# Attention and FFN block on one core: the VectorE's exponentials as five-pass cubics, in place of sums of five shifted bf16 patterns, with the FFN weights resident

## The chip, the cores and the metric

The kernel runs on one core of a Trainium2 chip. The core has a matrix engine (TensorE, PE in the profile), a vector engine (VectorE, DVE), an activation engine (ScalarE, ACT), GpSimd (POOL), SyncE (SP), which here issues nearly all transfers, and 16 DMA engines. Engines run their own instruction streams in order and meet at semaphores. SBUF is the on-chip memory, PSUM the accumulators that the PE writes. The metric is the device time of one execution in microseconds.

## What is computed

One block of a conditioned transformer, 2048 tokens, width 512, 32 heads of 16, FFN width 1792, all in bf16:

```
sa, ca, ga, sb, cb, gb = split(silu(c) @ w_mod, 6)
h = layernorm(x) * (1 + ca) + sa
q, k, v = h @ wqkv                                  # per head: [2048, 16]
x = x + ga * (softmax(q k^T / 4) v) @ wo
h = layernorm(x) * (1 + cb) + sb
x = x + gb * ((gelu(h @ w_gate) * (h @ w_up)) @ w_down)
```

The scores are 32 heads by 2048 by 2048, so 134 million exponentials. In tiles of 128 keys by 512 queries that is 2048 tiles.

## The kernel before

The scores are made transposed, keys on the partitions. Queries come in six sets (`SETS`: four of 512, 512, 512 and 256 queries, two of 128). A unit is four heads (every second head of a block of eight) times one query set; four score tiles of one unit that the PE can make side by side are a round. `qk` writes score tiles into PSUM `ps_sc`, six banks used as two halves of three. One ACTIVATE then reads up to three tiles at once, takes the exponential and writes bf16 tiles into E, a ring of slots. `pv_mms` multiplies a round of four tiles by V with a column of ones appended (`vaug`), in four column tiles side by side, and accumulates a whole unit in `ps_pv`. The ones give the softmax denominators. At a unit's end (`unit_end`) DVE copies the sums to `osb`; the denominators go through DRAM (`scr_den`, `scr_rec`) with six transfers on SP, a reciprocal on DVE lies between, and a multiplication gives `onorm`.

No order is written out by hand: a planner in `stream` emits it. It models each engine's free time and each operation's readiness, and at each step chooses the next PE work: three (or two) score tiles for the free half of `ps_sc`, a PV round, a piece of "side" work (projections, output projection, FFN, all in `ps_mi`), or a filler matmul that keeps the PE active. Side work follows the list in `plan`, with a start and a due position in score tiles; `credit` is how far it is behind. DVE work is queued as tasks and taken when the model has DVE free.

On top of this DVE makes exponentials of some score tiles. When the group of three has room and DVE is near free, one of the three banks holds a tile for DVE and the ACTIVATE covers two. Before the change, whole rounds of four go to DVE. Q is scaled so that a score is 65536 times the base-2 exponent. A single `tensor_scalar` from PSUM turns it into a uint16 that, read as bf16, is a piecewise linear power of two (`kq`), divided by five. `shift_task` adds four constants to these bits, one 2048-wide operation each (`sq`), which moves the joints of the linear pieces. The round then takes five PV passes: `kq` with `vaug`, and each shifted copy with `vs`, V scaled back by the shift. PSUM sums the five. Only rounds with key tiles from 12 on (`T0`) qualify, since `vs` holds no more. PV rounds may go out of order, and shift tasks have an urgency of their own.

SBUF is full with these buffers. So the FFN weights of the first four sets are streamed: `load` and `load_down` in `side_ffn` fetch 256-column blocks into two buffers each, on SP's queue, once per set. For the last sets `weight_parts` loads what remains resident, over the dead regions of qT, xs, dreg and mreg.

The split of a 128-column matmul into four 32-column tiles is in `mm` and is the same in both kernels:

```
if tp is None and int(rhs.ap[0][1]) == P and int(lhsT.ap[-1][1]) == P and mybir.dt.size(rhs.dtype) == 2:
    for j in range(4):
        self.mm(out[32 * j:32 * j + 32], lhsT[:, 32 * j:32 * j + 32], rhs, start, stop, (0, 32 * j))
```

Since all operations are recorded by helpers, the profile gives the helpers' lines: L309 is every matmul, L322 every ACTIVATE, L334 `tensor_scalar`, L339 `scalar_tensor_tensor`, L326 `tensor_tensor`, L343 copies, L372 every DMA. The groups are told apart by their tiles.

Of the kernel before, what the change touches and what calls it, by code (L numbers as in the profile page):

```python
# [13 lines left out]
P = 128  # L14
# [22 lines left out]
NSL = 12  # L37
assert NSL % CH == 0
LEAD = 5
T0 = 12  # L40
NK = 3
CREDIT = 1024
NS = 4
AHEAD = 24
FLOW = 4
URGENT = 9
LAG = 40
# [6 lines left out]
OCT = 65536.0  # L54
EXP_SCALE = float(np.log(2.0) / OCT)
Q_SCALE = float(0.25 * np.log2(np.e) * OCT)

SHIFT = (26, 51, 77, 102)
SHIFT_C = float(128 * (127 - np.log2(5) - 0.0565))
# [354 lines left out]
class _Kernel(_Recorder):  # L414
# [12 lines left out]
    def alloc(self):  # L427
# [8 lines left out]
        self.prodL = hreg[:, 0:NFC * 256].rearrange("p (f n) -> p f n", f=NFC)  # L436
# [6 lines left out]
        self.wst = [[mreg[:, 1024 * (2 * x + b):1024 * (2 * x + b) + 1024].rearrange("p (a n) -> p a n", a=NDC)  # L443
                     for b in range(2)] for x in range(2)]
        self.sq = [mreg[:, 4096 + 2048 * i:6144 + 2048 * i] for i in range(NS)]
        self.wmod = mreg[:, 0:NDC * 3072].rearrange("p (a n) -> p a n", a=NDC)
        dreg = sb("dreg", [P, NFC * D], BF16)
        self.tb1 = dreg[:, 0:8 * D].rearrange("p (b t n) -> p b t n", b=2, t=4)
        self.warm = dreg[:, 8 * D:9 * D]
        self.wdst = [dreg[:, a * D:(a + 2) * D] for a in (8, 10, 12)] + [mreg[:, a * D:(a + 2) * D] for a in (2, 0, 6, 4)]  # L450
        self.wdst = [a.rearrange("p (f n) -> p f n", f=2) for a in self.wdst]
        self.wg = [self.qT[:, :, 256 * i:256 * i + 256] for i in range(6)]
        self.wg.append(hreg[:, NFC * 256:NFC * 256 + 1024].rearrange("p (a n) -> p a n", a=NDC))
        self.wu = [self.wst[i // 2][i % 2] for i in range(4)]
        self.wu += [dreg[:, 1024 * i:1024 * i + 1024].rearrange("p (a n) -> p a n", a=NDC) for i in range(4, 7)]
        self.wd = [self.xs[:, 2 * i:2 * i + 2, :] for i in range(6)]
        self.wd.append(hreg[:, NFC * 256 + 1024:NFC * 256 + 2048].rearrange("p (f n) -> p f n", f=2))
        self.kq = [dreg[:, 0:2048], dreg[:, 2048:4096], mreg[:, 12288:14336]]
        self.vs = sb("vs", [P, len(SHIFT), NKT - T0, H * VW], BF16)
        self.wo = sb("wo", [P, 8, D], BF16)  # L460
        self.E = sb("E", [P, NSL, 512], BF16)
        self.onorm = sb("onorm", [P, 8, 512], BF16)
        self.ga = sb("ga", [P, D], BF16)
        self.gb = sb("gb", [P, D], BF16)
        self.xw = self.gw[:, 0, 0, 0:D]
# [11 lines left out]
        self.asum = self.rden[:, 0:2, 0:6]  # L477
        self.sc_bf = sb("sc_bf", [P, NDC], BF16)
        self.scbc = self.onorm[:, 0, :].rearrange("p (a n) -> p a n", a=NDC)
        self.modA = sb("modA", [P, 8], FP32)  # L480
        self.modB = sb("modB", [P, 8], FP32)
        self.rm4 = self.den[:, 0, 0:4]
        self.rm = sb("rm", [P, 2], FP32)
        self.ident = sb("ident", [P, P], BF16)
        self.ones = self.onorm[:, 1, 0:P]
# [8 lines left out]
    def prologue(self):  # L494
# [19 lines left out]
        self.memset(dve, self.ones, 1.0)  # L514
# [5 lines left out]
        self.memset(pool, self.rm4, 1.0)  # L520
        self.affine_select(self.rm4, [[-32, 4]], ALU.is_ge, 0.0, -16, 1)
        self.affine_select(self.rm4, [[32, 4]], ALU.is_ge, 0.0, 31, -1)
        self.reduce(self.rm[:, 1:2], self.rm4, mybir.AxisListType.X, ALU.add)
# [3 lines left out]
        for dc in range(NDC):  # L527
            self.mm(self.scp[:, 0, dc:dc + 1], self.crow[0:1, P * dc:P * dc + P], self.onorm[0:1, 1, 0:1])
# [28 lines left out]
    def act_stat(self, t):  # L557
        self.act(self.E[:, 0, :], self.xs[:, t, :], ACT.Copy, accum=self.asum[:, 0, t - 4:t - 3])
        self.act(self.E[:, 0, :], self.xs[:, t, :], ACT.Square, accum=self.asum[:, 1, t - 4:t - 3])
# [36 lines left out]
    def ln_norm(self, t, dst, src=None):  # L596
        self.ts("dve", dst, self.xs[:, t, :] if src is None else src, self.mv[:, t, 0:1], self.rstd[:, t:t + 1], ALU.subtract, ALU.mult)

# [89 lines left out]
    def side_v(self, g, dc):  # L688
        mi = self.mi[:, :]

        def part(t):
            for dci in range(NDC):
                self.mm(mi[:, P * t:P * t + P], self.hT[:, dci, 512 * g + P * t:512 * g + P * t + P],
                        self.wqkv[:, dci, 1024 + P * dc:1024 + P * dc + P],
                        start=(dci == 0), stop=(dci == NDC - 1))
        for t in range(4):
            yield 512, lambda t=t: part(t)
        dst = self.vaug[:, 4 * g:4 * g + 4, VW * 8 * dc:VW * 8 * dc + VW * 8]
        self.copy("dve", dst.rearrange("p t (h c) -> p t h c", c=VW)[:, :, :, 0:DH],
                  mi.rearrange("p (t h c) -> p t h c", t=4, c=DH))  # L700
        self.done(("v", g, dc))
        if 4 * g == T0 and not self.dry:
            c = slice(VW * 8 * dc, VW * 8 * dc + VW * 8)
            self.task([lambda i=i, o=o: self.ts("dve", self.vs[:, i, :, c], self.vaug[:, T0:NKT, c], float(2.0 ** (-o / 128)),
                                                None, ALU.mult) for i, o in enumerate(SHIFT)], ("vs", dc))
        yield END
# [60 lines left out]
    def side_mod(self):  # L767
        mi = self.mi[:, :]
        if not self.dry:
            self.task([lambda dc=dc: self.ts("dve", self.scbc[:, dc, :], self.ones, self.sc_bf[:, dc:dc + 1],  # L770
# [28 lines left out]
    def weight_parts(self):  # L799
# [3 lines left out]
        gv = self.B_w_gate.rearrange("(a p) n -> p a n", p=P)  # L803
        uv = self.B_w_up.rearrange("(a p) n -> p a n", p=P)
        dv = self.B_w_down.rearrange("(f p) n -> p f n", p=P)
        a = [part(self.wg[i], gv[:, :, 256 * i:256 * i + 256], "wg%d" % i) for i in range(7)]
        a += [part(self.wd[i], dv[:, 2 * i:2 * i + 2, :], "wd%d" % i) for i in range(7)]
        b = [part(self.wu[i], uv[:, :, 256 * i:256 * i + 256], "wu%d" % i) for i in range(7)]
        return a, b

    def up_w(self, w, fc, dci):
        return w[fc // 2][:, dci, P * (fc % 2):P * (fc % 2) + P]
# [15 lines left out]
    def normed(self, k, i):  # L828
        return self.E[:, NSL - 1, :] if k == len(SETS) - 1 else self.tb2[:, i, :]
# [5 lines left out]
    def wo_fin(self, bank, t):  # L835
        self.tt("dve", self.xw, bank, self.ga[:, :], ALU.mult)
        self.tt("dve", self.xs[:, t, :], self.xs[:, t, :], self.xw, ALU.add)

    def down_mm(self, bank, i, fc):
        self.mm(bank, self.prodL[:, fc, P * i:P * i + P], self.wd[fc // 2][:, fc % 2, :], start=(fc == 0), stop=(fc == NFC - 1))  # L840

    def down_fin(self, bank, t):
        self.tt("dve", self.xw, bank, self.gb[:, :], ALU.mult)
        self.tt("dve", self.xs[:, t, :], self.xs[:, t, :], self.xw, ALU.add)
        self.dma("sp", self.out[0, P * t:P * t + P, :], self.xs[:, t, :], "out%d" % (t % 4))

    def up_mm(self, bank, w, fc, c0, W, dci):
        self.mm(bank, self.up_w(w, fc, dci), self.t2T[:, dci, c0:c0 + W], start=(dci == 0), stop=(dci == NDC - 1))
# [35 lines left out]
    def side_ffn(self, gi, part=None):  # L884
# [6 lines left out]
        prod = self.prodT if W == 512 else self.prodL  # L891
        flow = gi < FLOW
# [6 lines left out]
        def load(x, ci):  # L899
            if flow and ci < len(chunks):  # L900
                v = (self.B_w_gate, self.B_w_up)[x].rearrange("(a p) n -> p a n", p=P)
                self.dma("sp", self.wst[x][ci % 2], v[:, :, 2 * P * ci:2 * P * ci + 2 * P], "st%d%d" % (x, ci % 2))

        def load_down(i):
            if flow:
                v = self.B_w_down.rearrange("(f p) n -> p f n", p=P)
                self.dma("sp", self.wdst[i], v[:, 2 * i:2 * i + 2, :], "sd%d" % i)

        yield from self.until(("ln2", gi))
        if flow:  # L910
            load(0, 0)
            load(1, 0)
        else:
            yield from self.until("weights")
        for h in range(2):
            yield from self.side_t(lambda t: self.normed(gi, t), n, h,
                                   lambda dc: self.t2T[:, dc, c0:c0 + W], self.modB)

        def up(x, ci, sub):
            for s, fc in enumerate(sub):  # L920
                for dci in range(NDC):
                    if flow:
                        lhs = self.wst[x][ci % 2][:, dci, P * (fc % 2):P * (fc % 2) + P]
                    else:
                        lhs = self.up_w((self.wg, self.wu)[x], fc, dci)
                    yield W, lambda s=s, lhs=lhs, dci=dci: self.mm(
                        mi[:, W * s:W * s + W], lhs, self.t2T[:, dci, c0:c0 + W], start=(dci == 0), stop=(dci == NDC - 1))

        def G(ci):
# [3 lines left out]
            load(0, ci + 1)  # L933
            for b0 in range(0, m, kpb):
                sub = fcs[b0:b0 + kpb]
                yield from up(0, ci, sub)
# [8 lines left out]
        def U(ci):  # L945
# [4 lines left out]
            load(1, ci + 1)  # L950
            for b0 in range(0, m, kpb):
                sub = fcs[b0:b0 + kpb]
                k = len(sub)
                yield from up(1, ci, sub)
                self.stt(w[:, W * b0:W * (b0 + k)], w[:, W * b0:W * (b0 + k)], 1.0, mi[:, 0:W * k], ALU.add, ALU.mult)
                if b0 + kpb >= m:
                    self.tt("dve", prod[:, fcs[0]:fcs[0] + m, c0:c0 + W], w.rearrange("p (k n) -> p k n", k=m),
# [3 lines left out]
        for i in range(3):  # L961
            load_down(i)
        for ci in range(nch + 1):
            if ci < nch:
                yield from G(ci)
                if ci >= nch - 2:
                    load_down(3 + ci - nch + 2)
            if ci >= 1:
                yield from U(ci - 1)
                if ci >= nch - 1:  # L970
                    load_down(5 + ci - nch + 1)
# [3 lines left out]
        for i in range(n):  # L975
            for fc in range(NFC):
                yield 512, lambda i=i, fc=fc: self.mm(
# [596 lines left out]
```

The softmax here doesn't subtract the row's maximum and nothing guards it: scores larger than these inputs give would overflow.

## Time and profile before

| | |
|---|---|
| Median of 3 runs | 906.21 us (904.66 to 907.97) |
| The profiled execution | 906.21 us, span 904.5 us |
| PE busy | 817.2 us (90%), 13408 matmuls |
| DVE busy | 687.5 us (76%), 1303 instructions |
| ACT busy | 841.9 us (93%), 747 instructions |
| DMA moved | 47.76 MB |
| Mean granted PE clock | 0.981 |

The span runs from the first to the last instruction in the profile. An engine's busy time is the union of its instructions' times, so instructions that overlap count once, and counts times means can exceed it. A busy PE is not a PE at its peak, as matmuls are pipelined. A group's line gives output and inputs, shapes, the count, then busy us and mean ns of one, and the idle time just ahead of the group on its engine with what ended it.

### The profile page before, as it was taken

The numbers are of one execution on the slowest core, as the hardware profiler recorded it, in microseconds if no ns is written. First come the engines' busy times: TensorE is split into PE (matmuls) and PEld (weight loads), VectorE is DVE, ScalarE is ACT, GpSimd is POOL, SyncE is SP. The second block draws the span as 40 slices with busy tenths as digits, with TensorE's granted clock in tenths as the row PEclk, the third lists the DMA queues.
The fourth block names the chain that finished last, engine by engine and source line by source line (L and its number), as shares of the span: only waits on it lengthen the run. The fifth ranks groups of instructions, "written<-read, shape, count | busy, mean of one in ns | idle before, by whom it ended". The sixth has DMA issues, their size and how long they took to land.

```text
span 904.5 us, 29537 instructions
## 1 busy us (share of the span) xinstructions
PE 817.2 (90%) x13408; PEld 288.4 (32%) x13408; DVE 687.5 (76%) x1303; ACT 841.9 (93%) x747; POOL 3.7 (0%) x11
## 2 busy tenths in 40 slices
PE   5898899999999999999999999999998899888885
PEld 2333232322232222222222222223432333345454
DVE  4854678988899889999898899888866744545372
ACT  3999899999999999999999999999999999978871
POOL 1000000000000000000000000000000000000000
PEclk7999899999999999999999999999999999979999
DMA  9000000000102111211003211110122221553400
GB/s 302 3 26 15 15 3 26 4 27 2 26 14 72 37 49 49 52 45 38 26 2 99 61 42 53 49 31 26 27 79 72 78 66 53 152 150 104 112 7 15
DMA packets 74935, 47.76 MB, mean 53 GB/s; under 512 B 17693, under 2 KB 70618, under 8 KB 74810
## 3 DMA queue, kind: packets, MB, share of 16 engines
q1 hardware_dynamic: 72426, 44.30, 16.9%
q8 instruction: 105, 1.72, 0.8%
q10 hardware_dynamic: 2384, 1.57, 0.6%
q14 instruction: 20, 0.16, 0.1%
HBM read 43.25 MB, written 2.61 MB: 51 GB/s over the span
## 4 chain that ended last, share of the span: by engine, by line
ACT 51%; PE 31%; DMA 7%; DVE 7%; SPq 3%; issue 2%; DVEq 0%
ACT E L322 49%; PE ps_mi L309 13%; PE ps_sc L309 12%; PE ps_pv L309 6%; DMA scr_rec<-rden 3%; SPq L372 3%; ACT wreg L322 2%; DMA mreg<-in_B_w_gate_dram 1%; DVE mreg L334 1%; DMA mreg<-in_w_mod_dram 1%; DVE wreg L326 1%; DVE wreg L339 1%; DVE wreg L343 1%; DMA rb<-scr_rec 1%; DMA mreg<-in_B_w_down_dram 1%
## 5 line engine op out<-in xcount | busy, mean ns | idle before, releaser
L322 ACT ACTIVATE E<-ps_sc 128x1536 bf16<-128x1536 f32 (+2 forms) x698 | 811.6, 1318 | 35.2 <-PE ps_sc L309 33.9
L309 PE MATMUL ps_sc<-qT,kmo 32*128 32x512 bf16 (+2 forms) x1408 | 183.8, 328 | 10.8 <-ACT E L322 7.5
L309 PE MATMUL ps_sc<-qT,kme 32*128 32x512 bf16 (+2 forms) x1344 | 178.0, 333 | 14.4 <-ACT E L322 12.1
L309 PE MATMUL ps_pv<-E,vaug 128*17 128x512 bf16 (+2 forms) x2380 | 175.7, 323 | 3.5 <-ACT E L322 1.7
L334 DVE TENSOR_SCALAR dreg<-ps_sc 128x512 uint16<-128x512 f32 x188 | 129.5, 690 | 36.0 <-PE ps_sc L309 34.0
L309 PE MATMUL ps_mi<-wreg,mreg 128*32 128x512 bf16 (+2 forms) x1920 | 124.1, 355 | 17.4 <-DVE wreg L339 5.4
L334 DVE TENSOR_SCALAR mreg<-dreg 128x2048 uint16<-128x2048 uint16 x188 | 123.1, 682 | 2.8 <-PE ps_pv L309 2.8
L309 PE MATMUL ps_pv<-mreg,vs 128*17 128x512 bf16 (+1 forms) x1232 | 98.4, 361 | 1.9 <-DVE mreg L334 1.4
L309 PEld LDWEIGHTS ps_sc<-qT,kme 32*128 32x128 bf16 x1344 | 46.6, 91 | 133.1 <-ACT E L322 92.6
L309 PEld LDWEIGHTS ps_sc<-qT,kmo 32*128 32x128 bf16 x1408 | 49.2, 93 | 121.7 <-ACT E L322 83.4
L309 PEld LDWEIGHTS ps_pv<-E,vaug 128*17 128x17 bf16 x2380 | 53.3, 89 | 91.3 <-issue 61.1
L334 DVE TENSOR_SCALAR mreg<-ps_sc 128x512 uint16<-128x512 f32 x92 | 63.0, 689 | 16.0 <-PE ps_sc L309 15.0
L309 PEld LDWEIGHTS ps_mi<-wreg,mreg 128*32 128x32 bf16 x1920 | 42.8, 98 | 73.9 <-issue 26.0
L334 DVE TENSOR_SCALAR mreg<-mreg 128x2048 uint16<-128x2048 uint16 x92 | 60.3, 684 | 0.9 <-PE ps_pv L309 0.9
L343 DVE CAST wreg<-ps_mi 128x512 bf16<-128x512 f32 x51 | 35.0, 686 | 23.9 <-PE ps_mi L309 23.3
L339 DVE SCALAR_TENSOR_TENSOR wreg<-wreg,ps_mi 128x512 bf16<-128x512 bf16 x51 | 34.9, 683 | 18.4 <-PE ps_mi L309 14.4
L309 PE MATMUL ps_sc<-xs,ident 128*32 128x512 bf16 x352 | 31.6, 401 | 11.4 <-ACT E L322 10.6
L309 PE MATMUL ps_mi<-hreg,wreg 128*32 128x512 bf16 x480 | 39.9, 391 | 0.7 <-DVE vaug L343 0.5
L309 PEld LDWEIGHTS ps_pv<-mreg,vs 128*17 128x17 bf16 x1232 | 29.4, 89 | 34.5 <-DVE mreg L334 16.6
L326 DVE TENSOR_TENSOR onorm<-osb,rb 128x512 bf16<-128x512 f32 (+2 forms) x43 | 23.6, 549 | 19.8 <-DMA rb<-scr_rec 19.6
L309 PE MATMUL ps_mi<-mreg,hreg 128*32 128x512 bf16 x448 | 36.5, 384 | 0.2 <-DMA mreg<-in_B_w_down_dram 0.2
L309 PE MATMUL ps_mi<-wo,onorm 128*32 128x512 bf16 x480 | 36.0, 387 | 0.7 <-DVE wreg L326 0.5
(136 smaller groups left out, 560.5 us busy)
## 6 DMA issues: line engine op xcount, KB each, us to landing
mreg<-in_B_w_up_dram SPq DMA_DIRECT2D x32, 256.0 KB, 3.4
mreg<-in_B_w_gate_dram SPq DMA_DIRECT2D x28, 256.0 KB, 3.3
rb<-scr_rec SPq DMA_DIRECT2D x96, 64.0 KB, 2.0
mreg<-in_B_w_down_dram SPq DMA_DIRECT2D x16, 256.0 KB, 2.8
dreg<-in_B_w_down_dram SPq DMA_DIRECT2D x12, 256.0 KB, 4.5
mreg<-in_w_mod_dram SPq DMA_DIRECT2D x1, 2048.0 KB, 14.3
out_dram<-xs SPq DMA_DIRECT2D x16, 128.0 KB, 1.8
rb<-scr_rec SPq DMA_DIRECT2D x52, 32.0 KB, 1.8
```

Source lines behind the costliest of these rows:

```text
L309: return self.rec("pe", lambda e: e.matmul(out, lhsT, rhs, start=start, stop=stop, tile_position=tp), [lhsT, rhs], [out], cost=(n, int(rhs ...
L322: return self.rec("act", lambda e: e.activation(out, in_, func, scale=scale, **kw), rd, wr, cost=self.cost("act", out, [in_], "act"))
L326: return self.rec(eng, lambda e: e.tensor_tensor(out, a, b, op), [a, b], [out], cost=self.cost(eng, out, [a, b], "tt"))
L334: return self.rec(eng, lambda e: e.tensor_scalar(out, a, s1, s2, **kw), rd, [out], cost=self.cost(eng, out, [a], "ts"))
L339: return self.rec("dve", lambda e: e.scalar_tensor_tensor(out, a, s, b, op0=op0, op1=op1), rd, [out], cost=self.cost("dve", out, [a, b], " ...
L343: return self.rec(eng, lambda e: e.tensor_copy(out, in_), [in_], [out], cost=self.cost(eng, out, [in_], "ts"))
L372: return e.dma_start(out, in_)
```

## The change

DVE's exponentials are made otherwise, one tile at a time:

```
 def exp_dve(self, i, bank):
     t, lo, u, out = self.dt[i % 2], self.dlo[i % 2], self.du[i % 2], self.ED[:, i % 3, :]
     return [lambda: self.ts("dve", t, bank, 127 * OCT, 0.0, ALU.add, ALU.max),
             lambda: self.stt(u, lo, EXP_C2 / EXP_C3 * OCT, lo, ALU.add, ALU.mult),
             lambda: self.stt(u, u, (EXP_C1 - 1) / EXP_C3 * OCT ** 2, lo, ALU.add, ALU.mult),
             lambda: self.ts("dve", t.bitcast(FP32), t, 128 / OCT, None, ALU.mult),
             lambda: self.stt(out.bitcast(I16), u, 128 * EXP_C3 / OCT ** 3, t.bitcast(FP32), ALU.mult, ALU.add)], out
```

The score becomes an int32 whose low half is the fraction; a cubic of the fraction corrects the linear power; the sum is written as the bits of a bf16 tile, `ED`. One PV pass uses it like a tile of E. Tiles are taken singly (the fourth of a round, some five groups ahead), with at most two in flight. PV rounds go strictly in order again. `vs`, `kq`, `sq`, the shift tasks and their urgency are gone, E has 15 slots for 12, and several small tensors that shared space have their own.

The room is used for resident FFN weights: `wg`, `wu` and `wd` lie whole in mreg and dreg and are loaded once with 12 transfers, one every eight score tiles, as soon as the modulation vectors are done. The streaming loads and the late loads are gone from `side_ffn`. The due position of the third FFN set moves from the end of the fourth set + 40 tiles to + 60 (`LAG`), that of the fourth from + 80 tiles to 16 tiles ahead of the end of the fifth.

The core of the diff:

```diff
-NSL = 12
+NSL = 15
-NS = 4
-LAG = 40
+NACT = 2
+LAG = 60
...
-        due = (ends[1] + 30, ends[2] + 30, ends[3] + LAG, ends[3] + 2 * LAG)
+        due = (ends[1] + 30, ends[2] + 30, ends[3] + LAG, ends[-2] - 16)
...
-        self.vs = sb("vs", [P, len(SHIFT), NKT - T0, H * VW], BF16)
+        self.wg = mreg[:, 0:NDC * F].rearrange("p (a n) -> p a n", a=NDC)
+        self.wu = mreg[:, NDC * F:2 * NDC * F].rearrange("p (a n) -> p a n", a=NDC)
+        self.wd = dreg[:, :].rearrange("p (f n) -> p f n", f=NFC)
+        self.ED = sb("ED", [P, 3, 512], BF16)
...
-        def load(x, ci):
-            if flow and ci < len(chunks):
-                v = (self.B_w_gate, self.B_w_up)[x].rearrange("(a p) n -> p a n", p=P)
-                self.dma("sp", self.wst[x][ci % 2], v[:, :, 2 * P * ci:2 * P * ci + 2 * P], "st%d%d" % (x, ci % 2))
...
-                if len(mem) == CH and "modB" in self.have and self.free["dve"] < t + 700:
...
+                if (('v', 3, 0) in self.have and len(active) < NACT and sum(v >= 4 * rp for v in vec) < 3
+                        and self.backlog() < BACK and self.free["dve"] < t + 700
+                        and len(mem) == CH and slack > -100 and self.credit < 1024):
+                    g = pos + CH * LEAD
+                    g += 3 - g % 4
+                    while g in vec:
+                        g += 4
...
-                    self.ts("dve", kq[:, 512 * j:512 * j + 512].bitcast(U16), self.scp[:, s0 + n, :], 128 / OCT, SHIFT_C,
-                            ALU.mult, ALU.add)
...
-                        for i in range(NS):
-                            self.shift_task(quad, i)
+                    steps, out = self.exp_dve(nd, self.scp[:, s0 + n, :])
+                    steps.pop(0)()
+                    self.task(steps, ("exp", nd))
+                    active.append((("exp", nd), g, out))
...
-            v = self.vs[:, i - 1, kt - T0, :] if i else self.vaug[:, kt, :]
             for j in range(4):
                 h = 8 * dc + 2 * j + ee
-                self.mm(acc[32 * j:32 * j + VW, 0:W], v[:, VW * h:VW * h + VW], src[j][:, W * kk:W * kk + W],
-                        start=first and kk == 0, stop=last and kk == kpb - 1, tp=(0, 32 * j))
+                self.mm(acc[32 * j:32 * j + VW, 0:W], self.vaug[:, kt, VW * h:VW * h + VW],
+                        self.slot[g0 + j][:, W * kk:W * kk + W],
+                        start=(kt == 0), stop=(kt == NKT - 1), tp=(0, 32 * j))
```

## The prediction

> **What bounds the kernel now.** I read the page's busy times first, then ACT's time slices, the chain of waits, the groups by shape, the stretches of 50 us, and last the waits inside the one stretch where ACT has gaps.
>
> The page, busy times and slices:
>
> ```profile
> PE 817.2 (90%) x13408; PEld 288.4 (32%) x13408; DVE 687.5 (76%) x1303; ACT 841.9 (93%) x747; POOL 3.7 (0%) x11
> ...
> ACT  3999899999999999999999999999999999978871
> ```
>
> ACT is full from the third slice until the last four. Stretches of 50 us (columns: stretch, length, PE, weight loads, DVE, ACT, POOL busy, clock, DMA share, GB/s):
>
> ```profile
> 200.00:250.00 50.00, 46.41 (x517) 12.38 (x517) 44.14 (x73) 50.00 (x49) 0.00 (x0) 1.00 0.06 16
> ...
> 750.00:800.00 50.00, 44.26 (x809) 17.94 (x804) 24.34 (x56) 45.82 (x38) 0.00 (x0) 0.93 0.43 126
> 800.00:850.00 50.00, 41.87 (x1103) 23.68 (x1099) 24.84 (x57) 44.69 (x37) 0.00 (x0) 0.93 0.35 100
> 850.00:900.00 50.00, 39.18 (x1485) 26.05 (x1482) 24.97 (x68) 26.41 (x27) 0.00 (x0) 0.97 0.14 36
> ```
>
> ACT lacks 904.5 − 841.9 = 62.6 us: 20.8 in the two stretches before 100 us (ACT busy 32.73 and 46.45 there), 4.2 over the 650 us from 100 to 750, 9.5 from 750 to 850, 28.1 after that, where the last FFNs drain. So for 650 us ACT alone sets the pace, and almost all of it is exponentials. The groups by shape (count, busy us, mean ns):
>
> ```profile
> L322 ACT ACTIVATE E<-ps_sc 128x1536 bf16<-128x1536 f32 x384 | 545.0, 1508 | 17.6 <-PE ps_sc L309 16.5
> L322 ACT ACTIVATE E<-ps_sc 128x1024 bf16<-128x1024 f32 x308 | 310.7, 1096 | 4.9 <-PE ps_sc L309 4.6
> ...
> L334 DVE TENSOR_SCALAR dreg<-ps_sc 128x512 uint16<-128x512 f32 x188 | 129.5, 690 | 36.0 <-PE ps_sc L309 34.0
> L334 DVE TENSOR_SCALAR mreg<-dreg 128x2048 uint16<-128x2048 uint16 x188 | 123.1, 682 | 2.8 <-PE ps_pv L309 2.8
> ...
> L309 PE MATMUL ps_pv<-mreg,vs 128*17 128x512 bf16 x1008 | 89.1, 380 | 1.9 <-DVE mreg L334 1.4
> ```
>
> 384 × 3 + 308 × 2 = 1768 of the 2048 score tiles are on ACT; the other 280 (188 + 92) are on DVE. An ACTIVATE over three tiles lasts 412 ns longer than one over two: that is the price of a tile on ACT. The PE's 90% is a pipelined engine's, and in 200 to 250 us ACT never waits for it.
>
> DVE's timeline, start and length, at 206 us and at 323 us:
>
> ```profile
> 206.26 0.68 DVE L334 TENSOR_SCALAR mreg<-mreg 128x2048 uint16<-128x2048 uint16 x1
> 206.86 0.68 DVE L326 TENSOR_TENSOR onorm<-osb,rb 128x512 bf16<-128x512 f32 x1
> 207.46 0.68 DVE L334 TENSOR_SCALAR qT<-ps_mi 128x512 bf16<-128x512 f32 x1
> ```
> ```profile
> 323.64 0.68 DVE L339 SCALAR_TENSOR_TENSOR wreg<-wreg,ps_mi 128x512 bf16<-128x512 bf16 x1
> 324.35 0.69 DVE L326 TENSOR_TENSOR hreg<-wreg 128x1024 bf16<-128x1024 bf16 x1
> ```
>
> Independent operations start 0.60 us apart although each lasts 0.68; one that reads the previous result starts 0.71 later.
>
> Waits from 790 to 826 us (us, times, longest):
>
> ```profile
> ACT E L322 <- PE ps_sc L309: 8.6, 4, 4.0
> ...
> PE ps_mi L309 <- DMA mreg<-in_B_w_gate_dram: 4.7, 2, 3.2
> ```
>
> The four long ACT gaps of that stretch are score tiles late because the PE, in order, stood in front of an FFN matmul whose streamed weight block had not landed. SP was late with it: its queue stood on the denominators' round trips (8.6 and 7.5 us on scr_rec and scr_den between 780 and 830).
>
> **What the Trainium skill says.** "ScalarE: Activation LUTs", what an exp ACTIVATE does: one element per cycle, 0.833 ns each for any function, 427 ns a tile; the trace has 412 (427 is an estimate, 512 × 0.833). "VectorE: DVE Perf Modes", the perf-mode tier table: tensor_scalar on 16-bit SBUF data runs 4×, on fp32 in SBUF 2×, anything two-input fp32 or from PSUM 1×. The trace agrees on two: 2048 16-bit elements last 682 ns, 512 from PSUM 690. It has no fp32 SBUF tensor_scalar of this size; the page's 1227 ns for 2048 gives by its own breakdown (150 + 8 + 256 cycles at 0.96 GHz) an estimate of 0.43 us for 512. "Perfetto Trace Analysis", identifying the most-contended engine: occupancy is a fair measure for ACT and DVE, not for the PE. That is how I treat 93% against 90%.
>
> **The change, part by part.** Counts are from the order in which the changed program issues its instructions.
>
> *Tiles move back to ACT.* DVE takes 162 tiles, not 280. ACT has 502 ACTIVATEs of three tiles and 190 of two: 1886 tiles in again 692 instructions. So 118 tiles × 0.412 = +48.6 us and no further start-up (at the skill's 0.427, +50.4).
>
> *DVE.* Removed: 280 first steps and 280 shifts, 376 us by their rows (129.5 + 63.0 + 123.1 + 60.3). Added per tile: one pass from PSUM, three scalar_tensor_tensor passes on 512 32-bit values, one fp32 tensor_scalar. At the independent spacing 4 × 0.60 = 2.4; the fifth is bounded by 0.34 (0.43 less the 0.08 overlap) and 0.60, and I take 0.34: 2.74 us a tile, 444 in all. DVE rises from 687 to some 790 us. Does it stay under ACT? I cut both programs every 46 exponentials and priced what each engine issues in a cut, 0.60 or 0.71 for DVE, 0.412 a tile plus 0.10 an instruction for ACT (the chain has 26 ACTIVATEs in 29.10 us). The fullest cut has 55.8 us DVE and 59.9 ACT; typical ones 49 to 53 against 55 to 58. DVE is hidden, but with only 4 to 6 us cover per cut, where before it had 5 to 10. The two chains in flight are mostly interleaved, so few successive operations depend on each other, and the first PV matmul reading a DVE tile comes in the order a median 3.4 us after the chain's work. I charge 3 us for chains that come late all the same: PV rounds now go in strict order, so a late one holds the rounds behind it, then the E slots, then the next ACTIVATE.
>
> *PE.* 1232 PV matmuls of the shifted terms go (98.4 us busy, four abreast). In their place come fillers: 309 of four matmuls, not 128, each about 0.4 us by its row, so some 72 us; the order puts one where ACT still has over 0.8 us of work ahead. ACT waits for the PE only 3.8 us from 100 to 750 us, so nothing comes back: 0, hidden under ACT; at most the 4.2 us.
>
> *Weights.* 84 streamed blocks (three weights, four sets, seven blocks each) and 21 late loads become 12 loads issued once behind the modulation. They share SP's queue with the first denominators, whose results are needed a whole set later: 0. The four gaps at 790 to 826 us lose their cause: −8.6, bounded by 0 (something else comes late there, as the denominators) and by the whole 9.5.
>
> *Layouts, due times.* Separate buffers for the small tensors and E with 15 slots cost no time. The fourth FFN is due 112 tiles later (tile 1984, not 1872). Past the last 46 exponentials both programs have 19 us of PE work and 15 to 16 of DVE, so the drain stays: 0, within ±4.
>
> Sum: 904.5 + 48.6 − 8.6 + 3 = 947.5 of span. The profiled execution took 906.21, 1.7 more than its span, and it is also the median of the three runs. 949.
>
> **The rivals.** *A: DVE becomes the bound.* If chains don't interleave (0.71, not 0.60, on four passes) a cut with 14 tiles needs 6 us more; if the fp32 pass runs at 1× another 3.6. With the first alone the cuts exceed ACT by 11 us together, with both by 39. 960 to 988, say 974. For it: the thin cover and the strict order. Against: the interleaving, and the skill's 2×.
>
> *B: the weight gaps stay in another form.* The denominators' round trips remain on SP, and the FFN of the fourth set now shares its time with more DVE tiles. Nothing is recovered: 904.5 + 48.6 + 3 + 1.7 = 958.
>
> *C: not slower.* ACT's waits were the crowded PE's, and without the 98.4 us of extra PV they vanish. It decides when more than 48.6 of ACT's 62.6 idle us go; all of it would give 892. Against: 20.8 lie in the prologue and 28.1 in the drain, where no shifted PV runs; all that is left is 13.7, and 906 + 48.6 − 13.7 = 941 is the floor I believe in.
>
> That the change is not what it says is excluded by the counts: 118 tiles do change engine.
>
> **How the numbers follow.** The sum as it stands 0.58 (own range 941 to 955), B 0.19 (954 to 963), A 0.20 (960 to 988), C 0.03. From 940 to 972 leaves out C and the upper half of A, and a little below: about 0.17. 0.3% of 906 is 2.7 us, about what a measurement can tell from no change; no case but C comes near it: slower 0.97, same 0.01, faster 0.02.
>
> **What would show it.** ACT busy near 890 us with 692 exponentials; the two-tile group at 190; ACT again 49 to 50 of 50 in the middle; DVE between 770 and 830; no DMA wait ahead of ACT late in the kernel. DVE's new rows: about 0.68 for the three long passes, near 0.43 for the fp32 one; 0.68 there speaks for A, as would ACT waiting on PE and PE on ED or dt in the middle. ACT gaps of 2 to 4 us past 750 would show B. I am wrong in the main if ACT's busy time grows by clearly other than 48, or its middle idle time is over 15 us.

## The result, and the profile after

The changed kernel takes 940.22 us in the median (939.15 to 941.34, four runs), the kernel before beside it 907.09 (904.66 to 909.09). The ratio is 1.0367, with a 95% interval of 1.0337 to 1.0396: slower by 33 us. The forecast was 949, 940 to 972: the direction and the main mechanism hold, the amount is some 9 us too large, and the result stands at the very edge of the range.

The page of the changed kernel, busy times and slices:

```profile
span 938.5 us, 28684 instructions
...
PE 791.4 (84%) x12900; PEld 267.2 (28%) x12900; DVE 787.5 (84%) x1537; ACT 887.9 (95%) x747; POOL 3.7 (0%) x11
...
ACT  3999999999999999998999999999999999999971
```

DVE was forecast at some 790 us and has 787.5. ACT was forecast near 890 and has 887.9, 46.0 more than before. What was not forecast in full is the other term: ACT's idle time fell from 62.6 to 50.6 us. Of the last five slices, 7, 8, 8, 7 and 1 tenths before, the first three now have 9; the last two, where the kernel drains, are as they were. Stretches (length, then PE, weight loads, DVE, ACT, POOL, clock, DMA share, GB/s):

```profile
200.00:250.00 50.00, 40.40 (x466) 9.97 (x463) 44.49 (x80) 50.00 (x43) 0.00 (x0) 1.00 0.05 13
...
750.00:800.00 50.00, 44.57 (x810) 15.82 (x802) 41.59 (x75) 50.00 (x42) 0.00 (x0) 1.00 0.06 13
800.00:850.00 50.00, 45.87 (x974) 20.43 (x974) 41.84 (x96) 49.95 (x42) 0.00 (x0) 1.00 0.08 22
850.00:900.00 50.00, 44.24 (x1260) 23.56 (x1256) 36.84 (x89) 49.66 (x41) 0.00 (x0) 1.00 0.07 16
```

ACT's idle time by stretch, before and after, worked out from such lines of one execution each. The changed kernel runs 34 us longer, so the same late work lies later in it; ACT's 49.66 of 50 us from 850 to 900 shows that the gaps have not just moved past 850.

| us of the span | before | after |
|---|---|---|
| 0 to 100 | 20.8 | 17.6 |
| 100 to 750 | 4.2 | 6.2 |
| 750 to 850 | 9.5 | 0.05 |
| 850 to the end | 28.1 | 26.8 |
| sum | 62.6 | 50.6 |

The groups by shape:

```profile
L314 ACT ACTIVATE E<-ps_sc 128x1536 bf16<-128x1536 f32 x502 | 723.8, 1592 | 8.1 <-PE ps_sc L301 8.1
L314 ACT ACTIVATE E<-ps_sc 128x1024 bf16<-128x1024 f32 x190 | 216.2, 1167 | 0.8 <-PE ps_sc L301 0.8
...
L326 DVE TENSOR_SCALAR dt<-ps_sc 128x512 int32<-128x512 f32 x162 | 111.8, 690 | 41.7 <-PE ps_sc L301 38.6
...
L331 DVE SCALAR_TENSOR_TENSOR ED<-du,dt 128x512 int16<-128x512 f32 x162 | 110.4, 683 | 0.8
L331 DVE SCALAR_TENSOR_TENSOR du<-dt 128x512 f32<-128x512 uint16 x162 | 109.7, 682 | 0.2
L331 DVE SCALAR_TENSOR_TENSOR du<-du,dt 128x512 f32<-128x512 f32 x162 | 109.5, 680 | 0.3
...
L326 DVE TENSOR_SCALAR dt<-dt 128x512 f32<-128x512 int32 x162 | 66.8, 416 | 0.5
```

The fp32 pass lasts 416 ns, where the forecast's estimate from the perf-mode tier table in the Trainium skill's "VectorE: DVE Perf Modes" was 0.43 us. It is the row that the kernel before did not have. That table's section gives 1× from PSUM for fp32 data, as here, and not for all data: its cap for `tensor_scalar` from PSUM is 2×.

From 790 to 826 us of the changed kernel, where ACT had its four gaps before, no ACT wait and no DMA is among the long waits; the PE waits for ACT instead, as it should:

```profile
PEld ps_sc L301 <- ACT E L314: 8.6, 21, 0.9
PEld ps_mi L301 <- issue: 4.2, 20, 0.2
```

### The profile page after: what moved, and what is told of

It is laid out like the page before. It is cut to its first block, busy times and chain, and to the rows that moved or that the text cites. A ratio compares the mean times of both kernels' runs of the same rounds, so it can differ in the third digit from the quotient of the medians.

```text
span 938.5 us, 28684 instructions
## 1 busy us (share of the span) xinstructions
PE 791.4 (84%) x12900; PEld 267.2 (28%) x12900; DVE 787.5 (84%) x1537; ACT 887.9 (95%) x747; POOL 3.7 (0%) x11
## 4 chain that ended last, share of the span: by engine, by line
ACT 80%; PE 9%; DVE 7%; DMA 2%; issue 2%; SPq 1%; DVEq 0%
ACT E L314 77%; PE ps_sc L301 4%; PE ps_mi L301 3%; ACT wreg L314 2%; PE ps_pv L301 1%; DVE du L331 1%; DMA scr_rec<-rden 1%; DVE xw L318 1%; DMA rb<-scr_rec 1%; DVE dt L326 1%; DVE st L354 1%; SPq L364 1%; DVE ED L331 1%; DMA xs<-in_A_x_dram 0%; DVE onorm L318 0%
## 5 line engine op out<-in xcount | busy, mean ns | idle before, releaser
L314 ACT ACTIVATE E<-ps_sc 128x1536 bf16<-128x1536 f32 (+2 forms) x698 | 860.8, 1467 | 19.7 <-PE ps_sc L301 19.6
L301 PE MATMUL ps_sc<-qT,kmo 32*128 32x512 bf16 (+2 forms) x1408 | 154.8, 324 | 26.8 <-ACT E L314 24.2
L326 DVE TENSOR_SCALAR dt<-ps_sc 128x512 int32<-128x512 f32 x162 | 111.8, 690 | 41.7 <-PE ps_sc L301 38.6
L301 PE MATMUL ps_sc<-xs,ident 128*32 128x512 bf16 x1132 | 93.5, 388 | 42.6 <-ACT E L314 41.3
L331 DVE SCALAR_TENSOR_TENSOR ED<-du,dt 128x512 int16<-128x512 f32 x162 | 110.4, 683 | 0.8
L331 DVE SCALAR_TENSOR_TENSOR du<-dt 128x512 f32<-128x512 uint16 x162 | 109.7, 682 | 0.2
L331 DVE SCALAR_TENSOR_TENSOR du<-du,dt 128x512 f32<-128x512 f32 x162 | 109.5, 680 | 0.3
L301 PE MATMUL ps_mi<-dreg,hreg 128*32 128x512 bf16 x840 | 71.5, 385 | 3.0 <-DVE xw L318 1.5
L326 DVE TENSOR_SCALAR dt<-dt 128x512 f32<-128x512 int32 x162 | 66.8, 416 | 0.5
L301 PE MATMUL ps_pv<-ED,vaug 128*17 128x512 bf16 (+2 forms) x199 | 61.7, 341 | 1.4 <-DVE ED L331 1.1
L335 DVE CAST wreg<-ps_mi 128x512 bf16<-128x512 f32 x51 | 35.1, 689 | 20.3 <-PE ps_mi L301 19.7
```

Source lines behind the costliest of these rows:

```text
L301: return self.rec("pe", lambda e: e.matmul(out, lhsT, rhs, start=start, stop=stop, tile_position=tp), [lhsT, rhs], [out], cost=(n, int(rhs ...
L314: return self.rec("act", lambda e: e.activation(out, in_, func, scale=scale, **kw), rd, wr, cost=self.cost("act", out, [in_], "act"))
L326: return self.rec(eng, lambda e: e.tensor_scalar(out, a, s1, s2, **kw), rd, [out], cost=self.cost(eng, out, [a], "ts"))
L331: return self.rec("dve", lambda e: e.scalar_tensor_tensor(out, a, s, b, op0=op0, op1=op1), rd, [out], cost=self.cost("dve", out, [a, b], " ...
L335: return self.rec(eng, lambda e: e.tensor_copy(out, in_), [in_], [out], cost=self.cost(eng, out, [in_], "ts"))
```

## The experiments

The theory is the forecast's sum: the time is ACT's tiles, less what late weight blocks cost before, and the PE's extra PV passes and DVE's work hide. The rivals are DVE as the bound (A), gaps that stay in another form (B), and a crowded PE (C).

**Fewer shifted rounds in the kernel before.** One edit takes DVE's share to the changed kernel's and leaves the streaming as it was; `KEEP` lists 40 of the 70 rounds:

```diff
-                if u not in units[:2] and r * (512 // u[3]) >= T0]
+                if u not in units[:2] and r * (512 // u[3]) >= T0 and g0 in KEEP]
```

> The kernel before, with only 40 of its 70 rounds of shifted exponentials left: 160 tiles on DVE, 1888 on ACT (504 ACTIVATEs of three tiles, 188 of two), as good as the changed kernel's 162 and 502/190; weights still streamed. If the tiles on ACT are the price: 120 x 0.41 = +49 us, 953 to 957. If the streamed weights' gaps are a matter of a crowded PE and vanish with fewer PV passes: 944 to 947. If DVE's chains or something else of the new exponentials cost time in the changed kernel, this one comes out below its 940.

951.96 us, ratio 1.0475 (1.0431 to 1.052), a little under the range. ACT's busy time is 891.5 us, 49.6 more for 120 tiles, or 0.413 each; its idle time, 63.3, is as before, though the profile is of the slowest of its four executions, 956.5 us. This kernel runs some 50 us longer than the one before, so its late work lies past 800 us, and there ACT is still short:

```profile
800.00:850.00 50.00, 37.66 (x767) 16.29 (x768) 19.53 (x51) 43.42 (x35) 0.00 (x0) 0.97 0.49 142
850.00:900.00 50.00, 40.68 (x1009) 20.85 (x1000) 19.14 (x43) 42.23 (x35) 0.00 (x0) 0.93 0.34 97
```

So the tiles are the price, fewer PV passes alone don't close the gaps, and the changed kernel is about 10 us faster than its number of tiles would make it (1.0475 against 1.0367 of 907; with both intervals, 5 to 15).

**No exponentials on DVE in the changed kernel.**

```diff
-                if (('v', 3, 0) in self.have and len(active) < NACT and ...
+                if (('v', 3, 0) in self.have and len(active) < 0 and ...
```

> The changed kernel with no exponentials on DVE: all 2048 tiles on ACT (664 ACTIVATEs of three, 28 of two, again 692), the 162 five-pass chains gone. If a tile on ACT costs 0.41 us and DVE's chains are hidden: 940 + 162 x 0.41 = 1006 to 1009. If DVE's chains hold the PE up in the changed kernel: less by what they hold it, 995 to 1004.

1003.58 us, ratio 1.109 (1.1043 to 1.1138). That is 63.4 us above the changed kernel by the medians, 0.39 per tile, and some 65.6 by the ratios, 0.405.

```profile
PE 827.3 (83%) x13524; PEld 276.6 (28%) x13524; DVE 345.9 (35%) x727; ACT 956.8 (95%) x747; POOL 3.7 (0%) x11
```

ACT is busy 68.9 us more for 162 tiles (0.425 each), and idle 45.4, or 5.2 less. The median lies inside the second statement, at its upper edge; the noise is too wide to tell the two statements apart. By one profile each, the chains cost ACT a few microseconds of waits: from 100 to 850 us ACT lacks 3.4 us here and 6.2 in the changed kernel, so about 3 of the 5.2 lie where the chains run. DVE's busy time shows what the chains take: 787.5 less 345.9 is 441.6 us for 162, or 2.73 each. The forecast had 2.74.

**The shifted copies left out of the kernel before.** `NS = 4` becomes `NS = 0`, and the 70 rounds stay the same.

> The kernel before, with the four shifted copies and their PV passes left out (DVE's 280 tiles keep only the first step and one PV pass, so their part of the softmax is wrong by a factor and a coarse power of two): 280 wide DVE operations and 1120 or so PV matmuls fewer, the same 1768 tiles on ACT. If ACT alone sets the pace: 901 to 908. If the crowded PE or DVE held ACT up: 890 or less.

907.12 us against 905.73, ratio 1.0016 (0.9989 to 1.0042).

```profile
PE 786.2 (87%) x12500; PEld 265.9 (29%) x12500; DVE 529.0 (58%) x1023; ACT 841.1 (93%) x747; POOL 3.7 (0%) x11
```

DVE falls from 687.5 to 529.0 us busy, the PE sheds 1232 PV matmuls (fillers take the place of some), and the time stays. Rival C is out: the PE's 90% and DVE's 76% in the kernel before held nothing up.

**Streamed blocks on another queue.** The 84 loads go to GpSimd's queue; the other engines' instructions are the same in the same order.

```diff
-                self.dma("sp", self.wst[x][ci % 2], ...
+                self.dma("pool", self.wst[x][ci % 2], ...
-                self.dma("sp", self.wdst[i], ...
+                self.dma("pool", self.wdst[i], ...
```

> The kernel before, with the 84 streamed weight blocks issued from GpSimd's queue instead of SP's; PE, ACT and DVE have the same instructions in the same order. If the gaps at 790 to 826 us come from SP's queue standing on the denominators' round trips: 8 to 10 us less, 896 to 899. If the gaps come from the denominators' own lateness or from the transfers themselves: 905 to 908. If GpSimd issues more slowly than SP: above 908.

902.06 us, ratio 0.9925 (0.9886 to 0.9964): a gain, of 7 us by the ratio with an interval of 3 to 10. The median lies between the statements, above the 896 to 899 of the first. Of the versions that do the whole work, it is the only one whose gain over the kernel before is clear of the noise. The four gaps from 790 to 826 us are gone but for small ones, yet ACT still lacks 5.8 us from 750 to 850.

**Late loads on that queue too.** `weight_parts` also issues from GpSimd.

> As the version with streamed blocks on GpSimd's queue, and the 21 late resident loads on it too. If the late loads also stand behind denominators on SP: another 1 to 4 us less, 893 to 897. If they are hidden: the same as that version within 1 us.

906.45 us, ratio 0.998 (0.9953 to 1.0006): neither statement, and 4 us above the version before it, with intervals that just overlap. ACT lacks 6.6 us from 750 to 850 and 30.2 after it. Why moving these loads gives the gain back was not settled.

**Streamed blocks loaded only once.** `load` and `load_down` get `and gi == 0`.

> The kernel before, with the streamed weights loaded for the first set of queries only; sets 2 to 4 use what lies in the buffers, so this part of the FFN is computed on wrong weights and the time of 63 transfers is left out. If late weight blocks cause the gaps: 895 to 898, as in the version on GpSimd's queue or a little below. If something else on SP or the PE is late there: 904 to 908.

900.54 us, ratio 0.9895 (0.9859 to 0.9931), above the 895 to 898 of the first statement. From 750 to 850 us ACT still lacks 8.1 us, of which 1.9 is a gap that in the kernel before opens at 849.8 us, at the stretch's end. The waits in this stretch show where the gap moved:

```profile
DVE onorm L326 <- DMA rb<-scr_rec: 20.1, 6, 8.3
...
PEld ps_mi L309 <- DVE wreg L339: 6.1, 7, 3.0
ACT E L322 <- PE ps_sc L309: 5.4, 5, 2.4
```

DVE stands on the denominators' last step, and what it has queued behind that is late: FFN values near 789 us, the copy of the next sums near 833. The PE stands on these in `ps_mi`, or on onorm itself near 847, and ACT's next input is late. In the changed kernel the same wait, onorm on rb, is 0.9 us in this stretch.

**No FFN weights loaded after the first set.** Additionally the late loads are left out.

> The kernel before with no FFN weights loaded after the first set: neither the 63 streamed blocks of sets 2 to 4 nor the 21 late resident loads (the FFN of all later sets is computed on whatever lies in the buffers). If the gaps that stayed past 750 us without reloads came from the late loads on SP's queue: 4 to 7 us below that version, 890 to 895, ACT full from 750 to 850 us. If they come from denominators' round trips alone, which VectorE waits for in order: the same as without reloads, 897 to 901, with onorm waiting on rb for 10 us or more from 750 to 850.

891.7 us, ratio 0.9803 (0.9777 to 0.9829). ACT is full from 750 to 850 us:

```profile
750.00:850.00 100.00, 89.21 (x2168) 43.96 (x2166) 56.88 (x137) 98.75 (x81) 0.00 (x0) 1.00 0.08 17
```

The first statement holds, by a little more than it said. Onorm still waits 11.3 us for rb, but this no longer reaches ACT. So of the kernel before, all FFN weight traffic after the first set cost 2.0%, about 18 us: some 9 came back without the reloads, the rest when the late loads went too. The late loads were not taken away alone. The profiled spans show about 15 (904.5 and 889.6): 8 in this stretch, 4 past it. The clock of the stretch rose with it, from 0.93 to 1.00; its share was not separated. Nor is it shown how the late loads cost their part: standing on SP's queue alone doesn't explain it, since moving them off that queue won nothing.

**Old due positions in the changed kernel.** `LAG = 40`, and the fourth FFN due at the fourth set's end + 80 tiles again.

> The changed kernel with the due positions of the third and fourth FFN as before (40 and 80 tiles behind the fourth set's end); 152 tiles on DVE, so 10 more on ACT, +4 us. If resident weights alone took the late gaps away: 943 to 946. If the later due position did it: the gaps of 9 us come back, 950 to 954.

939.96 us, ratio 1.0391 (1.0333 to 1.0449), with ten tiles more on ACT; the median is below the 943 to 946 of the first statement, and the interval reaches it.

```profile
750.00:850.00 100.00, 91.99 (x1806) 36.75 (x1807) 73.36 (x150) 99.99 (x82) 0.00 (x0) 1.00 0.07 18
```

The new due positions are not what closed the gaps. That resident weights are enough is read from this together with the kernel before without weight traffic, which closed them too; the 15 slots of E and the strict order of PV rounds were not tested apart.

**DVE's cover, taken away.** The second pass of each chain is issued twice in a first kernel, and in every other chain in a second. It writes the same values, so nothing is left out, and the planner counts it as free, so its order is made for less DVE work than there is.

```diff
-                lambda: self.stt(u, lo, EXP_C2 / EXP_C3 * OCT, lo, ALU.add, ALU.mult),
+                lambda: (self.stt(u, lo, EXP_C2 / EXP_C3 * OCT, lo, ALU.add, ALU.mult), self.again(u, lo)),
```

> The changed kernel with the second pass of each chain issued twice (the same values written again), which the planner counts as free; 156 tiles on DVE. DVE gets 0.71 x 156 = 111 us more, ACT 6 tiles (2.5 us). If DVE's cover is the 4 to 6 us of every 46 exponentials that I counted, ten cuts go over by 3 to 6 us: 975 to 990. If DVE had far more room than counted: 943 to 948. If DVE is the bound already: about 1040.

> The changed kernel with the second pass issued twice in every other chain: some 55 us more of VectorE work, 157 tiles on it (5 more on ACT, 2 us). If engine sums by cut decide (the cover of 4 to 6 us): 942 to 948, and the jump lies in the second half. If a late chain costs time as soon as VectorE is near full, since the PE stands in order on it: half of the 65 us of the full pass, 965 to 975.

The full version takes 1005.51 us, ratio 1.1096 (1.1031 to 1.1162): 65 us above the changed kernel for 108 us in the added row (156 of 692 ns; the expectation had estimated 111), well over the 975 to 990. The half version takes 954.96, ratio 1.0497 (1.0464 to 1.0531): 15 us above it by the medians, 12 by the ratios, for 54 us of added work and five more tiles on ACT. That is between its two statements. From 100 to 850 us, the changed kernel, the half and the full:

```profile
100.00:850.00 750.00, 638.54 (x9003) 190.82 (x9007) 667.64 (x1240) 743.75 (x611) 0.00 (x0) 1.00 0.07 20
```
```profile
100.00:850.00 750.00, 634.52 (x8741) 186.98 (x8739) 689.73 (x1269) 736.08 (x599) 0.00 (x0) 0.99 0.07 20
```
```profile
100.00:850.00 750.00, 617.48 (x7866) 174.72 (x7866) 694.44 (x1252) 696.35 (x561) 0.00 (x0) 0.94 0.06 18
```

DVE goes from 89.0% to 92.0% and then hardly further, 92.6%. In the full version ACT is busy 47 us less of these 750 than in the changed kernel. Taken over the whole stretch neither engine is full: DVE waits for scores, the PE stands in order on DVE's results, ACT waits for the PE, and the clock falls to 0.94.

But 92% is an average and no limit. Here are 50 us each of the changed kernel, of the half version, and two of the full version:

```profile
550.00:600.00 50.00, 41.89 (x497) 10.72 (x485) 47.51 (x84) 50.00 (x43) 0.00 (x0) 1.00 0.05 13
```
```profile
200.00:250.00 50.00, 41.57 (x466) 10.50 (x463) 48.84 (x88) 49.75 (x42) 0.00 (x0) 1.00 0.06 13
```
```profile
200.00:250.00 50.00, 41.74 (x422) 10.47 (x419) 48.57 (x86) 45.66 (x38) 0.00 (x0) 0.93 0.05 13
450.00:500.00 50.00, 41.11 (x418) 9.51 (x414) 44.58 (x79) 42.02 (x36) 0.00 (x0) 0.83 0.06 17
```

DVE reaches 95% in the first and 98% in the second while ACT is full or nearly so. In the full version there are stretches where DVE is all but full and ACT short, as rival A says, and others where DVE, at 89%, is not full and ACT is shorter still. Where between the changed kernel and the full version DVE becomes the bound can't be read from an average, and how much of the 65 us comes from an order planned without the added passes was not tested.

## Why the prediction was right, and where its sizes were off

*ACT sets the pace; a tile costs 0.412 us; +48.6 for 118 tiles.* Right. ACT's busy time rose by 46.0, by 49.6 for 120 tiles in the thinned kernel and by 68.9 for 162 without DVE's exponentials: 0.39, 0.413 and 0.425 a tile. By ACT's whole busy time the term is 2.6 us too large, but the exponentials' own group fits it:

```profile
L322 ACT ACTIVATE E<-ps_sc 128x1536 bf16<-128x1536 f32 (+2 forms) x698 | 811.6, 1318 | 35.2 <-PE ps_sc L309 33.9
```
```profile
L314 ACT ACTIVATE E<-ps_sc 128x1536 bf16<-128x1536 f32 (+2 forms) x698 | 860.8, 1467 | 19.7 <-PE ps_sc L301 19.6
```

That is 49.2 us more, 0.417 a tile. The rest of ACT's busy time, with the group's taken off, fell from 30.3 to 27.1, which no step of the forecast had. A closer price is in the last section.

*The late weight blocks, −8.6.* Late weight blocks did cost this, but the forecast had only part of the cause. Of its four gaps three (4.0, 1.9 and 2.3 us) have the PE on a weight block that had not landed; the fourth is 0.4. From 750 to 850 us 9.5 us came back, all that the stretch had lost, and this was the bound the forecast named but did not take. Rival B was half right: take the reloads away from the kernel before, and part of the gap comes back as a wait for denominators. It does not in the changed kernel. That the late resident loads cost as much as the streamed ones (0.9895 against 0.9803) was not in the forecast, which counted those 21 loads but priced only the streamed blocks' four gaps. So the size came out near its term with help from a part that it had not priced. (The forecast read ACT's slices as full until the last four; the digits fall below 9 in the last five. Its idle times don't depend on that.)

*Weight loads beside the first denominators: 0. Drain: 0, within 4.* The first 100 us lost 3.3 us less than before, which no step had. Of this 2.2 lie between 80 and 100 us, where the kernel before starts its shifted rounds and shows gaps of ACT on the PE and a clock of 0.90. Part of it is the chance of one execution: six other versions of the kernel before lose 18.9 to 20.7 us in the first 100, four of the changed kernel 17.2 to 18.2. The version without shifted copies is at the upper end of the first (20.7) and the changed kernel without DVE's exponentials at the lower end of the second (17.2), so neither the copies nor the five-pass chains are the cause; which of the other parts is stays open. The drain went from 28.1 to 26.8.

*DVE hidden, with 3 us for late chains.* Right: ACT's idle time from 100 to 750 us rose by 2.0, and without the chains ACT loses about 3 us less from 100 to 850. DVE's 790 came true as well (787.5), but not by the sum as written: 687 less 376 plus 444 is 755. The 376 adds up the rows, in which overlapping operations count in full; without any exponentials DVE is busy 345.9, so the old ones took 341.6 (taking DVE's other work as equal in both kernels), and 345.9 and 444 make 790. The cover was overrated, at least for an order that does not plan for the added work: counted by cuts, an added pass should have cost 35 to 50 us, and it cost 65.

*PE, 0.* Right, and shown by the kernel without shifted copies.

Together: 48.6 − 8.6 + 3 = 43.0 was forecast for the span. The profiled spans differ by 34.0: 46.0 of busy time, less 12.0 of idle time. The 9.0 between them are 2.6 from ACT's busy time, 0.8 past the 8.6 in the late stretch, 1.0 from the chains, 3.3 from the start and 1.3 from the drain. No step has the wrong sign. The forecast's own range of the likeliest case, 941 to 955, just misses the 940.2 because all five terms went one way. The measured time is also below the 941 that it called the floor it believed in. That 940.2 still falls inside the stated 940 to 972 is luck: it clears the edge by 0.2 us, less than the spread of the four runs. The sign and the main term are not luck.

## What to carry to other kernels

When one engine is full for most of the span, price a change by what it adds to that engine, then look for idle time of the same engine anywhere in the span that the change can hand back, and take the whole stretch's idle time as that term's upper end. Weights streamed on the queue that also carries small dependent round trips can arrive late behind them, as three of the gaps here did, and room freed by a costlier method can pay part of it back by making them resident. Don't take an average occupancy for a limit of a second engine: DVE ran at 95 to 98% in single stretches beside a full ACT, and yet, at 89% on average, 108 us of work that the order did not plan for cost 65 us, with the PE standing in order between the two.

## What was unexpected in the hardware's behaviour

The mean duration of an ACTIVATE is not its price. In the changed kernel the three-tile form lasts 1592 ns on average and the two-tile form 1167, against 1508 and 1096 before, though its speed is the same. With the union of both forms' times (811.6 and 860.8 us, which include some 5 us of smaller ones) and 0.412 us for the third tile, each of the 692 works out at 0.938 us for its first two tiles in both kernels. The start times in the two traces say it directly. Where one ACTIVATE on scores follows another without a gap, the median from start to start is 904 ns after one of two tiles in both kernels, and 1330 and 1331 ns after one of three. That is 427 ns a tile, just the forecast's estimate from the Trainium skill's "ScalarE: Activation LUTs" (what happens when an exp ACTIVATE runs), where the difference of the mean durations, 412, was somewhat low. What differs is the overlap in the records: its median after three tiles is 157 ns before and 271 ns in the changed kernel. That records grow where scores are ready early fits the shorter idle time ahead of the group (35.2 and 19.7 us), but was not tested.

A short stop of the PE and a lower clock came together. Between 376 and 390 us of the changed kernel the PE's weight loads wait 1.9 us for a DVE result in `ps_mi`, the granted clock from 380 to 390 is 0.83, and ACT then waits 2.3 us, the longest such gap of its middle part:

```profile
380.00:390.00 10.00, 7.72 (x83) 1.83 (x79) 8.07 (x16) 7.73 (x8) 0.00 (x0) 0.83 0.12 29
```

How much of the gap is the wait and how much the clock was not separated.
